# Cosformer attention into an MLP mixer on one core: the second batch's front re-ordered over three engines, num further from kv, and separate PSUM tiles for the last chunk's halves

## The chip, the core and the metric

The kernel runs on one core of a Trainium2 chip. A core has TensorE (PE; its weight loads are shown as PEld), VectorE (DVE), ScalarE (ACT), GpSimd (POOL) and SyncE (SP, which here only issues DMAs). Each engine works through its own queue in order and waits on semaphores for the others. The metric is the device time of one execution in microseconds; less is better.

## The reference

Inputs are q, k, v of (8 batches, 8 heads, 576 positions, 64) and four weights. Cosformer attention is linear attention with features `[relu(x) cos, relu(x) sin]` of width 128:

```python
kv  = einsum('bhsf,bhsd->bhfd', phi(k), v)        # 128 x 64 a head
z   = phi(k).sum(over s)
num = einsum('bhsf,bhfd->bhsd', phi(q), kv)
den = einsum('bhsf,bhf->bhs', phi(q), z) + 1e-6
x   = (num / den), heads side by side             # 576 x 512
u   = x + (relu(x.T @ w_tok1) @ w_tok2).T         # token mixing, 256 wide
out = u + relu(u @ w_ch1) @ w_ch2                 # channel mixing, 1536 wide
```

Inputs, weights and output are float32; matmul operands are bf16.

## The kernel before, in words

**Tiling.** A batch's 576 positions are four chunks of 128 (`ci` 0 to 3) and a tail of 64 (`ci` = R = 4); the tails of two batches share 128 partitions. Chunks are taken in `ORDER` 0, 1, 2, R, 3 from num on.

**Stages.** A batch has a *front* (class `Front`) and a *channel* (class `Channel`). Front: `k_side` and `q_side` make the features (two instructions a chunk, cosine and sine, L264 on DVE or L262 on ACT); `values` casts v into `v_aug`, which has a column of ones (L275 ACT, L277 DVE); q is transposed, for batches 0 and 1 by eight PE transposes and a copy (`q_trans`, L343, L347, L349), later by a DMA (`q_trans_dma`, L353); `kv` accumulates eight heads a chunk in one tile of two PSUM banks (L321) and `kv_out` copies the two halves to SBUF (L332); `num` multiplies (L362) and divides on DVE (L370 to L372); `mix_head` and `mix_tail` do w_tok1 (L385); `tok2` does w_tok2 and adds x (L409, L412), and casts to bf16 on ACT (L416, or L414 for the tail); `u_trans_dma` and `tail_trans_dma` (L438, L443) transpose u for the channel. Channel: twelve `c_step`s (relu(u @ w_ch1), L524 on PE, L528 on ACT; odd batches also do the two tails, L544), then `o_step`s of two matmuls each (L557), an addition on DVE (L562) and a store (L564).

**Interleaving.** The order of every queue is the order in which the Python calls are made. While batch b's channel runs, the front of batch b+1 is emitted in between: `pieces` makes a plan of (slot, what, chunk), where slot i is emitted after step i of the channel. C counts the twelve c steps (0 to 11), O the o steps (from 12). Batch 0's front runs alone (`first_front`) and leaves a special channel: its first three c blocks are done ahead, its `tok2` is not needed for the channel's input (which is built by matmuls), only for the final addition, and is emitted in slots 3 to 7.

**PSUM.** Two pools: `ps_mm`, four one-bank buffers (c, o, u, b), and `ps_at`, two buffers of two banks (kv, num, transposes).

**Loads.** All loads of q, k, v, all stores and all DMA transposes from batch 1 on are issued by SP in program order. Batch 2's k, v and q with their tails are issued after step 12 of batch 0's channel, behind a weight load. Batch 3's k follows at step 30.

The changed places are `values`, `kv_out`, `pieces`, `o_step` and the loop over batches at the end:

## Time and profile before

| | |
|---|---|
| median of 3 runs | 275.5 us (274.75 to 275.74) |
| the profiled execution | 275.3 us, span 273.5 us, granted clock 0.999 |
| PE / DVE / ACT / POOL busy | 263.8 / 163.8 / 128.8 / 9.6 us |
| matmul of 512 columns, between starts | 0.216 us |
| DVE feature, 128x512 (L264) | 0.45 to 0.48 us; 0.39 to 0.40 between starts |
| v cast on ACT, 128x512 (L275) | 0.59 us |
| copy of transposed q, 128x1024 | 1.00 us on ACT, 0.69 on DVE |
| k, q, v load of 1 MB, issue to landing (median) | 6.6, 9.0, 7.0 us |

How to read it: a timeline row has the start and the length in us, the engine, the source line, the operation and its operands, how many rows are merged, and in brackets the idle time of the engine before it and who ended it. Lengths of PE rows overlap, since matmuls are pipelined; the distance between starts is what a matmul costs. "SPq" rows are the issue of a DMA; its landing comes later. Batch 0's front ends at about 24 us, its channel runs to 60.3 us, batch 1's channel to about 93 us, and the following channels take about 28 (even) and 33 us (odd) each.

### The profile page before, as it was taken

The page shows a single profiled execution, that of the slowest core. Times are in us where ns is not written, and L with a number is a line of the kernel's source. Part 1 is how long each engine was busy: PE and PEld are TensorE (multiplying, and loading weights), DVE is VectorE, ACT ScalarE, POOL GpSimd, SP SyncE. Part 2 cuts the span into 40 slices and gives each one's busy share as a digit, 9 for nine tenths or more (in the row PEclk, how much of TensorE's full clock was granted, in tenths as well). Part 3 has the DMA queues.
Part 4 walks back from the last instruction along what each step waited for, and adds up shares of the span by engine and source line. Part 5 has one row for each costly group of instructions (what it writes and reads, how often), then busy time and mean ns, then how long its engine had stood idle before and what let it go on. Part 6 is the DMA issues. An engine that isn't in the chain of part 4 may idle for free.

```text
span 273.5 us, 5131 instructions
## 1 busy us (share of the span) xinstructions
PE 263.8 (96%) x2050; PEld 139.3 (51%) x2050; DVE 163.8 (60%) x374; ACT 128.8 (47%) x232; POOL 9.6 (4%) x22
## 2 busy tenths in 40 slices
PE   7989989989999999999999999999999999999993
PEld 3665446336654454446644455446644455445542
DVE  6963896779366467559366567759465666720121
ACT  4965871167616273347616272446615462525400
POOL 6400200000000000000000000000000000000000
PEclk9999999999999999999999999999999999999999
DMA  7999999968993989969784969579974371260032
GB/s 222 347 266 294 310 185 292 355 177 224 186 334 100 258 135 233 284 155 280 185 286 111 276 165 285 168 170 269 219 248 115 115 133 23 60 193 0 2 115 78
DMA packets 91816, 53.69 MB, mean 196 GB/s; under 512 B 59408, under 2 KB 86928, under 8 KB 91792
## 3 DMA queue, kind: packets, MB, share of 16 engines
q1 hardware_dynamic: 88432, 49.62, 66.3%
q0 software_dynamic: 2832, 3.21, 7.1%
q10 hardware_dynamic: 528, 0.52, 0.6%
q8 instruction: 16, 0.26, 0.4%
q14 instruction: 8, 0.07, 0.1%
HBM read 35.85 MB, written 9.44 MB: 166 GB/s over the span
## 4 chain that ended last, share of the span: by engine, by line
PE 85%; DVE 6%; ACT 3%; DMA 3%; issue 1%; POOL 0%; POOLq 0%; ACTq 0%
PE o_ps L557 31%; PE c_ps L524 24%; PE b_ps L385 6%; PE u_ps L409 6%; PE ct_ps L544 4%; PE idle_ps L205 4%; PE num_ps L362 3%; PE kv_ps L321 3%; DMA qpT<-qp 2%; DVE kp L264 1%; ACT qpT L347 1%; DMA uT<-u_bf 1%; ACT h1T L528 1%; DVE x_sb L372 1%; PE c_ps L534 1%
## 5 line engine op out<-in xcount | busy, mean ns | idle before, releaser
L557 PE MATMUL o_ps<-w_ch,h1T 128*128 128x512 bf16 (+1 forms) x396 | 95.1, 372 | 0.5 <-DVE o_sb L562 0.5
L524 PE MATMUL c_ps<-uT,w_ch 128*128 128x512 bf16 (+2 forms) x384 | 92.5, 372 | 0.9 <-DMA uT<-u_bf 0.9
L528 ACT ACTIVATE h1T<-c_ps 128x512 bf16<-128x512 f32 x93 | 55.5, 599 | 57.9 <-PE c_ps L524 57.7
L557 PEld LDWEIGHTS <-h1T 128*128 128x128 bf16 x396 | 37.1, 98 | 40.0 <-issue 1.5
L524 PEld LDWEIGHTS <-w_ch 128*128 128x128 bf16 x384 | 33.1, 97 | 30.1 <-DMA uT<-u_bf 1.4
L562 DVE TENSOR_TENSOR o_sb<-o_ps,u_sb 128x512 f32<-128x512 f32 (+1 forms) x33 | 22.2, 673 | 37.7 <-PE o_ps L557 35.7
L412 DVE TENSOR_TENSOR u_sb<-u_ps,x_sb 128x512 f32<-128x512 f32 x32 | 22.1, 689 | 9.7 <-PE u_ps L409 9.6
L416 ACT CAST u_bf<-u_sb 128x512 bf16<-128x512 f32 x28 | 17.3, 618 | 17.6 <-DVE u_sb L412 17.6
L390 ACT ACTIVATE B<-b_ps 128x512 bf16<-128x512 f32 x8 | 4.8, 597 | 39.6 <-PE b_ps L385 39.5
L409 PE MATMUL u_ps<-B,w_tok 128*128 128x512 bf16 x80 | 22.8, 379 | 0.1
L372 DVE TENSOR_TENSOR x_sb<-num_ps,den 128x512 bf16<-128x512 f32 x28 | 19.4, 691 | 1.0
L370 DVE TENSOR_SCALAR den<-num_ps 128x8 f32<-128x8 f32 (+1 forms) x35 | 5.8, 166 | 23.3 <-PE num_ps L362 23.1
L544 PEld LDWEIGHTS <-w_ch 128*128 128x128 bf16 x192 | 14.0, 98 | 9.2
L385 PE MATMUL b_ps<-x_sb,w_tok 128*128 128x512 bf16 x64 | 17.9, 379 | 0.0
L544 PE MATMUL ct_ps<-uT_tail,w_ch 128*128 128x128 bf16 x192 | 17.2, 219 | 0.0
L264 DVE TENSOR_SCALAR qp<-qt,cos_t 128x512 bf16<-128x512 f32 (+1 forms) x35 | 16.1, 459 | 0.6 <-DMA qt<-in_q_dram 0.6
L264 DVE TENSOR_SCALAR qp<-qt,sin_t 128x512 bf16<-128x512 f32 (+1 forms) x35 | 15.8, 451 | 0.0
L275 ACT CAST v_aug<-vt 128x512 bf16<-128x512 f32 (+1 forms) x28 | 15.7, 590 | 0.1
L362 PEld LDWEIGHTS <-qpT 128*128 128x128 bf16 x256 | 11.6, 98 | 7.6 <-issue 2.1
L264 DVE TENSOR_SCALAR kp<-kt,cos_t 128x512 bf16<-128x512 f32 x32 | 15.2, 479 | 0.4 <-DMA kt<-in_k_dram 0.4
L362 PE MATMUL num_ps<-kv_sb,qpT 128*128 128x65 bf16 x256 | 13.5, 193 | 1.4 <-DVE x_sb L372 0.5
L562 DVE TENSOR_TENSOR o_sb<-o_ps,u_tail 128x512 f32<-128x512 f32 x4 | 2.8, 692 | 19.2 <-PE o_ps L557 19.2
(93 smaller groups left out, 227.9 us busy)
## 6 DMA issues: line engine op xcount, KB each, us to landing
out_dram<-o_sb SPq DMA_DIRECT2D x31, 256.0 KB, 3.0
kt<-in_k_dram SPq DMA_DIRECT2D x7, 1024.0 KB, 6.6
qt<-in_q_dram SPq DMA_DIRECT2D x7, 1024.0 KB, 9.0
vt<-in_v_dram SPq DMA_DIRECT2D x7, 1024.0 KB, 7.0
w_ch<-in_moe_w_ch_dram POOLq DMA_DIRECT2D x4, 384.0 KB, 10.0
w_ch<-in_moe_w_ch_dram POOLq DMA_DIRECT2D x3, 512.0 KB, 8.3
out_dram<-o_sb SPq DMA_DIRECT2D x10, 128.0 KB, 2.3
qtt<-in_q_dram SPq DMA_DIRECT2D x8, 128.0 KB, 7.0
```

The source lines that it names most:

```text
L264: nc.vector.tensor_scalar(o_ap, i_ap, scalar1=w, scalar2=0.0, op0=ALU.mult, op1=ALU.max)
L362: nc.tensor.matmul(num_ps[:, g, j * DP:j * DP + D1], self.qT_of(ci, h), self.kv_sb[g][:, j, 0:D1], start=True, stop=True)
L372: nc.vector.tensor_mul(self.x_of(ci)[rows].rearrange("p (g j d) -> p g j d", g=2, j=HH), nv[:, :, :, 0:D], den.to_broadcast([rows.stop - r ...
L385: nc.tensor.matmul(self.b1_ps[mi], w, self.x_of(ci), start=(ci == ORDER[0]), stop=(ci == ORDER[-1]))
L409: nc.tensor.matmul(u_ps, w_tok2[:, ki, ci * P:(ci + 1) * P], self.B1[:, ki, :], start=(ki == 0), stop=(ki == NT - 1))
L412: nc.vector.tensor_add(u, u_ps[rows], self.x_of(ci)[rows])
L416: nc.scalar.copy(self.ub[:, ci, :], u)
L524: nc.tensor.matmul(c_ps[:, lo:hi], w_ch1[:, ki, mi * P:(mi + 1) * P], uT[:, lo // P:hi // P, ki, :], start=(ki == 0), stop=(ki == NCC - 1))
L528: nc.scalar.activation(self.h1T[:, mi, :], c_ps, AF.Relu)
L544: nc.tensor.matmul(self.ct_ps[:, mi % R, :], w_ch1[:, ki, mi * P:(mi + 1) * P], self.tail.uT[:, ki, :], start=(mi % R == 0 and ki == 0), s ...
L557: nc.tensor.matmul(o_ps, h, w_ch2[:, ki, cols], start=ki == 0, stop=ki == NCH - 1)
L562: nc.vector.tensor_add(o_sb, o_ps, u)
```

## The change

Five edits.

1. *Batch 1's front.* In `pieces` the plan for `first` is new. k features go to slots 4 to 7, q features 0 to 2 and transposes 0 and 1 to slots 8 to 10, and everything else up to kv stands in slot 11, the last c slot: q features 3 and R with their sine on ACT, transposes 2, 3 and R alternating with batch 0's `tok2` of chunks 2, 3 and R (now from `ps_mm`), v casts of chunks 0 and 1 on GpSimd, 2 and 3 on ACT, R on DVE, all of kv, and `kv_out`. Batch 0's `tok2` 0 and 1 go to slots 5 and 7. The nums move from O+4, 6, 7, 9, 10 to O+1, 3, 5, 7, 9, `mix` from O+11 to O+10, and the last `tok2` and the DMA transposes one slot earlier. Transposes 2 and R are copied on DVE, the others on ACT.
2. *kv_out* copies half 0 on ACT and half 1 on DVE, for every batch (before: both on ACT; batch 1 both on DVE), and in batches 2 to 7 stands one slot earlier, in the slot of the last kv.
3. *num of odd batches* from batch 3 on: the third, fourth and fifth num, `mix`, `tok2` and the transposes move one slot later.
4. *o_step* of the last batch's last chunk, done in two column halves, takes a PSUM tile for each half instead of one for both.
5. *Load of batch 2's q* (with its two tails) is issued after step 28 instead of step 12, behind the stores and DMA transposes of the steps between, with no wait on the weight load of its own.

```diff
-                nc.vector.tensor_copy(dst, src)
+                eng.tensor_copy(dst, src)
...
-        def kv_out(self, halves=(0, 1), eng=None):
-            copy = nc.scalar.copy if eng is None else eng.tensor_copy
+        def kv_out(self, halves=(0, 1)):
             for g in halves:
+                copy = nc.vector.tensor_copy if g else nc.scalar.copy
...
             if first:
-                plan = [(C + at, KS, ci, 0 < ci < R) for ci, at in enumerate((3, 4, 5, 5, 6))]
-                plan += [(C + at, QS, ci) for ci, at in enumerate((6, 7, 8, 8, 9))]
-                plan += [(C + at, QT, ci, (0, H), nc.vector if ci == R else nc.scalar)
-                         for ci, at in enumerate((9, 10, 11, 12, 13))]
-                plan += [(C + at, V, ci, nc.vector) for ci, at in enumerate((10, 11, 11, 11, 11))]
-                plan += [(O + at, KV, ci) for ci, at in enumerate((1, 1, 1, 2, 2))]
-                plan.append((O + 2, self.kv_out, (0, 1), nc.vector))
+                last = NCH - 1
+                plan = [(4, KS, 0), (5, KS, 1, True), (6, KS, 2, True), (6, KS, 3, True), (7, KS, R),
+                        (8, QS, 0), (9, QS, 1), (9, QT, 0), (10, QS, 2), (10, QT, 1)]
+                plan += [(last, *what) for what in (
+                    (QS, 3, True), (QT, 2, (0, H), nc.vector), (before.tok2, 2, None, False),
+                    (QS, R, True), (QT, 3), (before.tok2, 3, None, False),
+                    (QT, R, (0, H), nc.vector), (before.tok2, R, None, False))]
+                plan += [(last, V, ci, eng) for ci, eng in enumerate(
+                    (nc.gpsimd, nc.gpsimd, nc.scalar, nc.scalar, nc.vector))]
+                plan += [(last, KV, ci) for ci in range(NSC)]
+                plan.append((last, self.kv_out))
+                plan += [(5, before.tok2, 0, ps_at, False), (7, before.tok2, 1, ps_at, False)]
...
-                plan.append((C + (7 if odd else 8), self.kv_out))
+                plan.append((C + (6 if odd else 7), self.kv_out))
             if first:
-                at, mix, t = (O + 4, O + 6, O + 7, O + 9, O + 10), O + 11, O + 14
+                at, mix, t = (O + 1, O + 3, O + 5, O + 7, O + 9), O + 10, O + 14
             elif odd:
-                at, mix, t = (C + 8, C + 9, C + 10, C + 11, O + 2), O + 3, O + 7
+                at, mix, t = (C + 8, C + 9, C + 11, O + 1, O + 3), O + 4, O + 8
...
-            plan += [(t + at, T, ci) for ci, at in enumerate((0, 1, 2, 3, 3))]
-            plan += [(t + 2, self.u_trans_dma, 0, 3), (t + 3, self.u_trans_dma, 3, R)]
+            plan += [(t + at, T, ci) for ci, at in enumerate((0, 1, 2, 3, 3) if not first else
+                                                             (0, 0, 1, 2, 2))]
+            plan += [(t + 3 - first, self.u_trans_dma, 3, R)]
+            plan.append((t + 2 - first, self.u_trans_dma, 0, 3))
...
-            if lo == 0 and cols.start == 0:
+            if lo == 0:
                 self.o_ps[ci] = ps_mm.tile([P, Dm], F32, name="o_ps", tag="mm")
...
             if b == 0 and i == NCH:
-                load_batch(2, "kvq", behind=w_ch2_done[1])
+                load_batch(2, "kv", behind=w_ch2_done[1])
+            if b == 0 and i == NCH + 16:
+                load_batch(2, "q")
```

9 lines of the change are left out of this document (3 added, 6 removed).

## The prediction

> **What bounds the kernel now.** I read the page first, then the chain of waits in order of time, then the timeline engine by engine wherever the chain leaves TensorE (PE).
>
> ```profile
> PE 263.8 (96%) x2050; PEld 139.3 (51%) x2050; DVE 163.8 (60%) x374; ACT 128.8 (47%) x232; POOL 9.6 (4%) x22
> ...
> PEclk9999999999999999999999999999999999999999
> ...
> PE 85%; DVE 6%; ACT 3%; DMA 3%; issue 1%; POOL 0%; POOLq 0%; ACTq 0%
> ```
>
> PE sets the end, at a granted clock of 0.999. No PE work is added or removed, so the change is worth exactly the PE stalls that it takes away or makes. I measure a stall as the distance between two matmul starts, less the undisturbed distance: 0.216 us for 512 columns, 0.45 for a chunk's eight transposes, 0.243 for eight kv and 0.25 for eight num matmuls. From 26.6 us to the end, all stalls over 0.04 us:
>
> ```profile
> 39.71 0.61 PE L343 MATMUL qT_ps<-ident,qp 128*128 128x128 bf16 x8 [0.35 <-ACT qpT L347]
> ...
> 42.01 0.89 PE L321 MATMUL kv_ps<-v_aug,kp 128*128 128x65 bf16 x24 [0.30 <-ACT qpT L347]
> ...
> 50.08 0.38 PE L385 MATMUL b_ps<-x_tail,w_tail 128*128 128x512 bf16 x1 [0.26 <-DVE x_tail L372]
> ...
> 60.34 2.79 PE L524 MATMUL c_ps<-uT,w_ch 128*128 128x384 bf16 x24 [0.88 <-DMA uT<-u_bf]
> ```
>
> (a) Stage of batch 0 up to kv, 34.8 to 42.0: 0.21 + 0.07 + 0.41 + 0.51 + 0.51 + 0.47 = 2.17 us, transposes and kv behind their copies. From kv to 60.34: 0.20 + 0.42 + 0.26 + 0.11 + 1.05 = 2.04 (nums too close, then the wait for uT).
>
> ```profile
> 163.00 0.66 ACT L332 CAST kv_sb<-kv_ps 128x260 bf16<-128x260 f32 x2
> ...
> 163.43 0.56 PE L362 MATMUL num_ps<-kv_sb,qpT 128*128 128x65 bf16 x8
> ...
> 104.02 0.42 PE L362 MATMUL num_ps<-kv_sb,qpT 128*128 128x65 bf16 x8 [0.22 <-DMA qpT<-qp]
> ```
>
> (b) In the fronts of batches 3, 5 and 7 the first num waits for the copies of kv, which stand on ACT behind a relu: 0.26 + 0.16 = 0.42 each. Batch 3 loses 0.39 more to a late transposed q.
>
> ```profile
> 267.66 0.42 DVE L562 TENSOR_TENSOR o_sb<-o_ps,u_sb 128x256 f32<-128x256 f32 x1 [0.62 <-PE o_ps L557]
> 268.14 1.47 PE L557 MATMUL o_ps<-w_ch,h1T 128*128 128x256 bf16 x12 [0.52 <-DVE o_sb L562]
> ```
>
> (c) The last half chunk waits 0.57 for the addition that reads the other half of its tile. Batch 1's stage, 60 to 93, has no stall.
>
> **The change, part by part.** Sums are against the profiled execution's 275.3 us (span 273.5 and 1.8 around it), 0.2 under the median 275.5.
>
> *Batch 1's front up to kv.* The order of instructions gives each queue. PE starts c3 at 26.59 as before; seven c blocks (0.864) and two u (0.43) end at 33.50. The first transposes need q features 0, which DVE reaches at 32.66, after u_sb1; two at 0.396 would end by 33.5, two at the 0.65 spacing that the same kind shows at 33.38 and 34.04, while POOL issues its w_ch2 loads, by 33.95. I take a stall of 0.25. Then PE does T0, c10, T1, c11, T2, u2 by 37.3. T3 needs its sine on ACT, behind T0 copy, h, T1 copy, h (0.90 + 0.49 + 0.90 + 0.49 from 34.4, then a sine of 0.80): 38.0, so 0.8 lost. T3, u3, TR, uR end at 39.8.
>
> kv 0 and 1 need POOL's two casts. They start when vt lands, at 35.6. No cast on POOL is in the trace; below, half of its 0.95 us memset of 1024 elements gives 0.48, above, four times its 0.29 us select of 128 gives 1.16. Even 2.3 us for both ends at 37.9, two before kv: cost nothing. What hides them is PE's way to kv, and then the wait of kv 2; past 41.9 each microsecond would be one lost. kv 2 and 3 need casts on ACT that are queued behind ub_tail, and that waits for DVE: T_R copy until 40.45, u_tail until 41.1; ub_tail 0.53, casts 0.53 and 0.59: 42.3 and 42.8. PE came to kv 2 at 40.3, so 2.0 + 0.3 are lost, and kv ends at K = 43.4. (With DVE undelayed 43.15, delayed 43.6.) Stalls up to kv: about 3.4 where there were 2.17.
>
> *From kv to the next stage.* The kv copies: ACT, and then DVE, since the order has DVE wait for ACT's copy: 0.2 + 0.38 + 0.05 + 0.38 + 0.05 = 1.06 after K; four o matmuls and half a num (0.99) hide all but 0.08. Nums now come every 1.11 (four o, one num), just over DVE's 1.03 to 1.07 for one (0.20 + 0.24 + 0.60 to 0.67): 0.20 and 0.42 go. B is ready at K + 9.99, u reaches it at K + 10.1: 0.26 and 0.11 go. Third u_bf at K + 13.25; a uT transfer lands 3.3 later (56.98 to 60.29), so the next stage starts at S = K + 16.7, and PE has waited 0.75 instead of 1.05. S = 60.1 against 60.34: **-0.25** (0 to -0.5).
>
> *q of batch 2 behind the transposes.* This moves three DMAs past two stores and three transposes on SP. Before, q was issued at 47.73 and landed 8.3 us later, long ahead. Now it follows transposes of 1.51, 1.23 and 1.22 us (4.2 with gaps) from K + 13.3, so at K + 17.5 = S + 0.8. The next k load, two stores and the qpT transposes queue behind it. For a 1 MB load the rows next to it (kt and vt with nothing ahead of them) give 6.0, 6.2, 6.0, 6.4 and 6.6 to landing, behind another load 8.3 to 10.0; I take 6.2 since nothing stands ahead: S + 7.0. DVE is in order: q features 0 stand ahead of k features 3, which are ready 1.74 later (four at 0.396, write and signal) at S + 8.74. PE wants them for kv 3 at S + 7.93 (68.27 in the trace): 0.8 lost. The DVE half of kv_out stands behind fourteen features: S + 7.03 + 5.54 + 0.44 = S + 13.0, wanted at S + 12.6: 0.4 lost; the first qpT, behind k and two stores (2.7 + 0.7 + 0.7 + 0.7 for qtt, then 0.9), at S + 12.7, lies inside it. The second may cost 0 to 0.7; I take 0.2. **+1.4** (0 to +2.8).
>
> *kv_out a step earlier, half on DVE, later nums in odd fronts.* kv of batch 5 ends at 161.44; ACT's copy stands behind one relu until 161.9 and ends at 162.3, DVE's at 162.7; num comes at 163.17. Both waits go: 2 x 0.42 = **-0.84**. In batch 3 the next num waits for qpT, landed at 103.97, anyway: **-0.2** (0 to -0.8). Mix and uT move one slot (0.43) later; the closest uT, of batch 7, landed 1.1 ahead of use: nothing. Even fronts had no stall, and DVE is free 0.65 or more before num there. Batch 0's half on DVE ends when ACT's did (0.38 each).
>
> *Own banks for the last halves.* **-0.57**.
>
> Sum: 275.3 - 0.25 + 1.4 - 0.84 - 0.2 - 0.57 = **274.8 us**.
>
> **A rule weighed.** DVE's features slowed from 0.48 to 0.64 and 0.72 us while POOL issued loads at 32.28 to 34.51. The Trainium skill (SBUF — State Buffer, Who interferes with whom) says that DVE and GpSimd share a port pair, that a DVE cast or tensor_scalar in a two-port mode and a GpSimd instruction exclude each other, and that the first holds it for its whole length. By that, the last cosine before T3 would wait behind both casts until 37.9 and end at 38.4, T3 would be 0.4 later, and the sum 275.2; the rows here show only a slowing of 0.26 an instruction.
>
> **The rivals.**
> 1. Slower: q of batch 2 lands as late as queued loads did (8.3 to 9.0 us; 10.0 at most). For it: k of batch 3 is issued 2.6 us after it, and the page's median for qt is 9.0. Against: nothing is ahead of it. Every microsecond over 6.2 falls on kv 3: 276.9 to 277.6. It makes the change a loss from 6.9 us on, and one of over 0.5% from 8.3.
> 2. Faster: q lands in time. At 5.4 us (512 KB took 4.6 to 5.2) kv 3 does not wait and only the 0.4 at num are left, at 5.0 nothing: 273.4 to 273.8, so 273.6. For it: the rings are almost idle then. Against: no 1 MB row is under 6.0.
> 3. The odd fronts gain nothing, because DVE's half waits for ACT's half, which a relu still holds: 275.6. The order shows the wait; the times above leave 0.4.
> 4. POOL's casts outlast their cover. Each must take over 3.1 us, nearly three times my upper bound; at 4.5 us the second ends at 44.6 and kv at 45.6: 277.0. Against: all of POOL's rows but its loads are under 1 us.
>
> **How the numbers follow.** Chances: forecast 0.40, rival 1 0.20, rival 2 0.27, rival 3 0.06, rival 4 0.07. About 0.5% (1.4 us) is what a measurement of this kernel tells from no change: 274.1 to 276.9 around the median. A third of the forecast's own spread (274.0 to 275.8: batch 3's 0.6 down and 0.2 up, K's 0.25, qpT's 0.5 up) I put under 274.1. Faster: 0.13 + 0.27 = 0.40. Slower: 0.20 + 0.04 = 0.24. Same: 0.36. The range runs from 273.0 (rival 2 with batch 3's whole gain) to 277.2 (the middle of rival 1).
>
> **What would show it.** Right: kv 2 of batch 1 waits 2 us for an ACT cast, with ub_tail ahead; DVE idles between k features 2 and q features 0 of batch 2, and kv 3 there starts 0.8 late; no wait ahead of the first num of batches 5 and 7; the last twelve matmuls follow without a stop. Wrong: the stage of batch 1 without a stall, or casts on POOL of over 2 us, or kv of batch 1 ending before 42.5.

## The result and the profile after

The changed kernel takes 276.7 us (median of 11 runs, 275.45 to 278.54) where the kernel before takes 275.5 (11 runs, 274.75 to 275.91): ratio 1.0056, 95% interval 1.0032 to 1.0081. It is slower by 0.56%. The forecast was 274.8; the time lies inside its range and on the other side of no change. Three of the 11 executions had a mean granted clock of 0.993 to 0.994 and took 278.1 to 278.5; the other eight have a median of 276.55.

The first profile is of the execution that took 275.45 (span 273.6), the shortest of the 11. These are the lines of its page that answer to those of before: busy time, granted clock and the engines of the chain that ended last.

```profile
PE 261.6 (96%) x2050; PEld 138.7 (51%) x2050; DVE 164.7 (60%) x375; ACT 129.8 (47%) x229; POOL 11.2 (4%) x24
...
PEclk9999999999999999999999999999999999999999
...
PE 80%; DMA 7%; DVE 7%; ACT 2%; issue 1%; SPq 0%; DVEq 0%
```

PE has no more work than before. In the chain its share fell from 85% to 80%, and that of DMA rose from 3% to 7%: transfers have come into the path. The places, in order of time, from the timeline of PE (start, length, engine, line, operation, merged rows, and in brackets the idle time and who ended it):

```profile
34.44 0.62 PE L343 MATMUL qT_ps<-ident,qp 128*128 128x128 bf16 x8 [0.68 <-DVE qp L264]
...
38.76 0.62 PE L343 MATMUL qT_ps<-ident,qp 128*128 128x128 bf16 x8 [0.65 <-ACT qp L262]
...
42.95 0.92 PE L321 MATMUL kv_ps<-v_aug,kp 128*128 128x65 bf16 x16 [1.65 <-ACT v_aug L275]
...
69.03 0.42 PE L321 MATMUL kv_ps<-v_aug,kp 128*128 128x65 bf16 x8 [0.38 <-DVE kp L264]
...
73.70 0.42 PE L362 MATMUL num_ps<-kv_sb,qpT 128*128 128x65 bf16 x8 [0.75 <-DMA qpT<-qp]
...
243.80 2.55 PE L531 MATMUL c_ps<-uT,w_ch 128*128 128x512 bf16 x11 [0.61 <-DMA uT<-u_bf]
...
263.76 6.24 PE L564 MATMUL o_ps<-w_ch,h1T 128*128 128x512 bf16 x40
```

The first three are batch 1's front: T0, T3 and kv 2. The next two are batch 2's front: kv 3 and the first num. The sixth is new: batch 7's channel waits for its transposed u. The last row shows the end without a stop. No row of a first num in batches 5 and 7 has a bracket any more.

Beside it stands the same kernel profiled a second time (277.25 us, span 275.4; run e1 below). The table divides the spans by the starts of the channels, read from the timeline of PE: from batch 0's first mix matmul (L385) to batch 1's channel, then the length of each channel, with the next batch's front in it.

| stretch | before | forecast | after, first | after, second |
|---|---|---|---|---|
| start to batch 0's mix | 18.87 | no change | 18.76 | 19.55 |
| batch 0's mix to batch 1's channel | 41.47 | -0.25 | 41.80 (+0.33) | 41.98 (+0.51) |
| channel 1 (front of batch 2) | 32.79 | +1.4 | 34.26 (+1.47) | 34.35 (+1.56) |
| channel 2 (front of batch 3) | 28.31 | -0.2 | 27.78 (-0.53) | 28.01 (-0.30) |
| channels 3 and 5 | 32.75, 32.75 | no change | 32.74, 32.75 | 32.75, 32.75 |
| channel 4 (front of batch 5) | 27.91 | -0.42 | 27.47 (-0.44) | 27.47 (-0.44) |
| channel 6 (front of batch 7) | 27.91 | -0.42 | 28.25 (+0.34) | 28.74 (+0.83) |
| channel 7 to the last matmul | 26.59 | -0.57 | 25.92 (-0.67) | 25.92 (-0.67) |

Two stretches went against the forecast, batch 1's front and channel 6; channel 1 came out as forecast. The two profiles of one kernel differ by 0.8 in the start, which the change doesn't touch, and by 1.0 in stretches whose end waits for transfers. Over all twenty profiles of this document the start runs from 18.76 to 19.55, with a median of 19.0, so the first profile has the shortest start and the second the longest.

### The profile page after: what moved, and what is told of

Its sections match the earlier page's. It is cut to its first block, busy times and chain, and to the rows that moved or that the text cites. A ratio compares the mean times of both kernels' runs of the same rounds, so it can differ in the third digit from the quotient of the medians.

```text
span 273.6 us, 5130 instructions
## 1 busy us (share of the span) xinstructions
PE 261.6 (96%) x2050; PEld 138.7 (51%) x2050; DVE 164.7 (60%) x375; ACT 129.8 (47%) x229; POOL 11.2 (4%) x24
## 4 chain that ended last, share of the span: by engine, by line
PE 80%; DMA 7%; DVE 7%; ACT 2%; issue 1%; SPq 0%; DVEq 0%
PE o_ps L564 31%; PE c_ps L531 23%; PE b_ps L385 6%; PE u_ps L409 5%; PE num_ps L362 4%; PE ct_ps L551 4%; DMA qpT<-qp 4%; PE kv_ps L321 3%; DVE qp L264 2%; DMA uT<-u_bf 2%; DMA qt<-in_q_dram 2%; DVE kp L264 2%; PE idle_ps L205 1%; PE c_ps L541 1%; DVE u_sb L412 1%
## 5 line engine op out<-in xcount | busy, mean ns | idle before, releaser
L385 PE MATMUL b_ps<-x_sb,w_tok 128*128 128x512 bf16 x64 | 17.9, 379 | 0.0
L275 ACT CAST v_aug<-vt 128x512 bf16<-128x512 f32 (+1 forms) x30 | 16.7, 586 | 0.1
L321 PE MATMUL kv_ps<-v_aug,kp 128*128 128x65 bf16 x256 | 12.5, 193 | 2.2 <-ACT v_aug L275 1.7
```

What stands on the lines that cost most here:

```text
L321: nc.tensor.matmul(self.kv_ps[g][:, j * DP:j * DP + D1], self.k_of(ci)[:, g * HH + j, :, :] .rearrange("p a b -> p (a b)"), self.va[:, ci, ...
L385: nc.tensor.matmul(self.b1_ps[mi], w, self.x_of(ci), start=(ci == ORDER[0]), stop=(ci == ORDER[-1]))
```

## The experiments

Each run is given by median and runs, and by its ratio to the kernel before on the same chip. Theory D says that transfers have come into the path. Theory C says that the wait at kv 2 makes the chip grant TensorE less clock for a while.

### The changed kernel again (e1)

The edit: none.

> The changed kernel once more, with nothing altered, for a second profile and a second set of times. In its first profile the stalls of PE add up to a time of 275.45 us, while its median was 276.7; this run is to catch what differs between executions. Theory D (a DMA has come into PE's path): the times scatter between 275.4 and 277.5, and where a profile is longer than the first (span 273.6), its extra time stands at waits that end with a DMA: kv 3 of batch 2 behind q (0.55 before), the num of batch 2 behind the transposed q (0.91), the transposed u of batch 7 (0.78); the granted clock is 1.00. Theory C (the clock): the extra time, up to 2 us, stands in matmuls at a longer distance than 0.216 us, in one window shortly behind the stalls that PE has ahead of kv in batch 1 (33 to 43 us), where the row of the granted clock shows less than 9; the mean granted clock is 0.993 to 0.996.

277.33 us (12 runs, 276.57 to 278.52), ratio 1.0057 [1.0027, 1.0087]; two executions had a clock of 0.994. The timeline of PE in its profile:

```profile
70.37 0.42 PE L321 MATMUL kv_ps<-v_aug,kp 128*128 128x65 bf16 x8 [0.74 <-DVE kp L264]
...
74.77 0.42 PE L362 MATMUL num_ps<-kv_sb,qpT 128*128 128x65 bf16 x8 [0.47 <-DMA qpT<-qp]
...
245.59 1.69 PE L531 MATMUL c_ps<-uT,w_ch 128*128 128x512 bf16 x7 [1.11 <-DMA uT<-u_bf]
```

kv 3 waits longer than in the first profile (0.74 against 0.38), num less, the transposed u longer (1.11 against 0.61); the clock is 1.00. This is theory D's picture, with 0.8 at the start that no theory had.

### One part of the change at a time (e12, e4, e6, e5)

e12 is the kernel before with batch 1's new front alone, which the sum had at -0.25.

```diff
+                last = NCH - 1
+                plan = [(4, KS, 0), (5, KS, 1, True), (6, KS, 2, True), (6, KS, 3, True), (7, KS, R),
...
+                plan.append((last, self.kv_out, (0, 1), True))
...
-                at, mix, t = (O + 4, O + 6, O + 7, O + 9, O + 10), O + 11, O + 14
+                at, mix, t = (O + 1, O + 3, O + 5, O + 7, O + 9), O + 10, O + 14
```

> The kernel before with batch 1's new order of pieces alone (its copies on three engines, batch 0's tok2 among them, its nums and transposes one slot earlier); q of batch 2 early, kv_out, the odd batches and the last chunk as before. My sum had -0.25 for it: 275.2. The profiles have the next stage start later instead of earlier, counted from batch 0's mix: 39.8 and 40.0 in the changed kernel and 40.2 with q early, where the kernel before has 39.5; so +0.3 to +0.75, and with three executions in ten at a lower clock the median may gain 0.3 more: 275.7 to 276.5.

276.48 us (12 runs, 274.89 to 278.11), ratio 1.0022 [0.9994, 1.005]; four executions had a clock of 0.991 to 0.994. From batch 0's mix to batch 1's channel it takes 41.63, 0.16 more than before; the other stretches are within 0.23 of before. That profile is of one of the shortest executions (275.02). The eight executions at full clock have a median of 275.65, 0.4 over the kernel before on the same chip (275.27), and the four at a lower clock raise the median by 0.8 more. So the front looks like a loss, not the small gain of the sum, though its ratio's interval still touches no change.

e4 is the kernel before with own tiles for the last halves and the earlier, split kv_out.

```diff
+                copy = (eng.tensor_copy if eng is not None else
+                        nc.vector.tensor_copy if g and len(halves) == 2 else nc.scalar.copy)
...
-                plan.append((C + (7 if odd else 8), self.kv_out))
+                plan.append((C + (6 if odd else 7), self.kv_out))
...
-            if lo == 0 and cols.start == 0:
+            if lo == 0:
```

> The kernel before with two parts of the change alone: an own PSUM tile for each half of the last chunk, and in batches 2 to 7 the copies of kv one slot earlier, the second half on DVE. Batch 1's front, the nums of odd batches and the loads stay as before. My sum's terms: -0.57 at the end, -0.42 each in batches 5 and 7, -0.2 in batch 3 (0 to -0.8): 273.9, between 273.5 and 274.5, against 275.5. If the earlier copy only moves a wait (the next num then waits for DVE, since the nums are not spread), one or both of the 0.42 stay and the time is 274.3 to 274.9. If DVE's half holds up other DVE work, even batches lose up to 0.4 each and the time is 275 or over.

273.88 us (12 runs, 273.3 to 275.31), ratio 0.9923 [0.9891, 0.9954]: the number forecast. In its profile the end has -0.68, and batches 5 and 7 have -0.41 each; batch 3 has -0.04 instead of -0.2, and batch 1's front, which the edit doesn't touch, -0.18. The first nums of batches 5 and 7 start without a wait although the nums stand as before, so the shift of the odd batches was not needed for this gain.

e6 is the kernel before with the late load of q alone.

```diff
-                load_batch(2, "kvq", behind=w_ch2_done[1])
+                load_batch(2, "kv", behind=w_ch2_done[1])
+            if b == 0 and i == NCH + 16:
+                load_batch(2, "q")
```

> The kernel before with the late load of batch 2's q alone. By the changed kernel's rows the late q costs 0.55 + 0.91 = 1.46 in one profile, 0.91 + 0.63 = 1.54 in the other, and taking it back moved the median by 2.0. Theory: 275.4 + 1.5 to 2.0 = 276.9 to 277.4, with waits at kv 3 and at a num of batch 2 that end with the load of q and its transpose. Rival: the transposes of batch 1 stand later in this kernel's order than in the changed one, so q is issued later still, up to 1 us: 278. Other rival: the cost belongs to the changed front, and here it is under 0.5.

281.86 us (6 runs, 281.18 to 283.47), ratio 1.024 [1.0215, 1.0265]: a miss by over 4 us. SP's queue in its timeline shows what was overlooked:

```profile
57.13 1.39 SPq L438 DMA_TRANSPOSE uT<-u_bf  x1
58.57 0.57 SPq L86 DMA_DIRECT2D qt<-in_q_dram  x1
59.19 1.38 SPq L92 DMA_DIRECT2D qtt<-in_q_dram  x2
60.67 0.57 SPq L564 DMA_DIRECT2D out_dram<-o_sb  x1
61.33 3.08 SPq L438 DMA_TRANSPOSE uT<-u_bf  x1
```

Batch 1's last transposes are one step later in the old front, so step 28 puts the 1 MB load of q between the two transposes of u. The second lands at 67.43, and PE waits for it:

```profile
67.47 1.44 PE L524 MATMUL c_ps<-uT,w_ch 128*128 128x128 bf16 x12 [4.77 <-DMA uT<-u_bf]
```

That q lands at 65.41 and the store behind it at 66.93, so here a transpose that stands behind a 1 MB load in SP's order landed behind it. And all six executions had a clock of 0.987 to 0.994. The windows of the same profile (stretch, its length, busy time and rows of PE, PEld, DVE, ACT, POOL, then granted clock, DMA share, GB/s):

```profile
65.00:66.00 1.00, 0.00 (x0) 0.00 (x0) 0.56 (x2) 0.00 (x0) 0.00 (x0) 0.71 1.72 263
66.00:67.00 1.00, 0.00 (x0) 0.00 (x0) 1.00 (x3) 0.00 (x0) 0.00 (x0) 0.50 0.99 138
...
72.00:73.00 1.00, 1.00 (x11) 0.59 (x9) 0.00 (x0) 0.12 (x1) 0.00 (x0) 0.88 1.23 252
```

PE stands still from 62.7. Some 2.7 us later the clock falls to 0.50 and stays there until about 72.2, and matmuls of 512 columns then stand 0.427 apart instead of 0.216. Channel 1 is 7.19 longer than before: 4.9 for the stall, and 2.3 for the matmuls at half clock behind it.

e5 is the changed kernel without the one-slot shift of the odd batches.

```diff
-                at, mix, t = (C + 8, C + 9, C + 11, O + 1, O + 3), O + 4, O + 8
+                at, mix, t = (C + 8, C + 9, C + 10, C + 11, O + 2), O + 3, O + 7
```

> The changed kernel with the one-slot shift of the odd batches' later nums, mix, tok2 and transposes undone, nothing else. My sum had that shift at nothing; the two profiles of the changed kernel show the channel of batch 7 waiting 0.78 and 1.27 for the transposed u, where the kernel before had no wait. Theory (a store has come between the two transposes because of the shift): the wait goes, and as the run with the early copies of kv and unshifted nums had no wait ahead of the nums of batches 5 and 7, nothing comes back: 0.8 to 1.3 less, 275.6 to 276.4 where the changed kernel has 276.7 and 277.3. Rival: the late q of batch 2 has shifted the queue of transfers for good, and batch 7 waits for the transposed u all the same: 276.7 to 277.3.

276.62 us (12 runs, 275.13 to 278.54), ratio 1.0057 [1.0034, 1.008]. In its profile channel 6 is 27.50 and the wait for batch 7's transposed u is gone, as expected; the ratio is the changed kernel's all the same. Five of the twelve executions had the lower clock (277.0 to 278.5); the other seven have a median of 276.3, where the other runs of the changed kernel have 276.55 and 277.19. The same edit is cleaner between two kernels without such executions, e3 and e11 below: ratios 0.9985 and 0.996, 0.7 less (the intervals, [0.9957, 1.0012] and [0.9932, 0.9988], overlap). So the profiles show the wait come and go with the shift, and the medians bear out its price only weakly. Why the shift costs it is in SP's queue: in the changed kernel a store stands between the two transposes of u, in the kernel before it does not. The changed kernel:

```profile
238.12 2.05 SPq L438 DMA_TRANSPOSE uT<-u_bf  x1
240.27 0.52 SPq L571 DMA_DIRECT2D out_dram<-o_sb  x1
241.23 1.20 SPq L438 DMA_TRANSPOSE uT<-u_bf  x1
```

The kernel before:

```profile
237.41 3.21 SPq L438 DMA_TRANSPOSE uT<-u_bf  x2
240.74 1.20 SPq L443 DMA_TRANSPOSE uT_tail<-ub_tail  x1
```

The second transpose, issued at 239.43 before and at 241.23 now, lands at 243.76 instead of 241.78, with channel 7 due at 243.0. The two traces differ by 0.71 at the start of channel 6, so the issue has to be counted back from the moment at which channel 7 could start (242.75 before, 243.03 now): it stood 3.32 ahead of it and now stands 1.80 ahead. Of these 1.52, 0.43 is the slot, 0.96 the time from the begin of the store to the second issue, and 0.13 the first transpose's longer issue.

### Repairs of the changed kernel, one at a time (e2, e3)

e2 loads batch 2's q after step 12 again.

```diff
-                load_batch(2, "kv", behind=w_ch2_done[1])
-            if b == 0 and i == NCH + 16:
-                load_batch(2, "q")
+                load_batch(2, "kvq", behind=w_ch2_done[1])
```

> The changed kernel with batch 2's q loaded after step 12 again, behind k and v, as in the kernel before. My sum had +1.4 for the late q; the first profile of the changed kernel shows 0.55 ahead of kv 3 and 0.91 ahead of the first num of batch 2. Theory D: both waits go, and with them the scatter, the median falls by 1.5 to 2.3 us, from 276.7 to 274.4 to 275.2, at or under the kernel before's 275.5. Theory C: the same 1.5 go in every execution, but executions with a granted clock of 0.993 to 0.994 that are some 2 us longer stay as frequent as they were (3 of 11). Rival: q takes the rings from k and v again, so that k and v of batch 2 land later and the front of batch 2 waits for them instead; then the median stays within 0.5 of 276.7.

275.28 us (12 runs, 274.48 to 276.79), ratio 0.9983 [0.9954, 1.0012], 2.05 under e1 beside it. Channel 1 is back at 32.78. The executions with a lower clock did not go: four of twelve, 275.9 to 276.8.

e3 issues the v casts of batch 1 ahead of the last two tok2.

```diff
-                    (QS, R, True), (QT, 3), (before.tok2, 3, None, False),
-                    (QT, R, (0, H), nc.vector), (before.tok2, R, None, False))]
-                plan += [(last, V, ci, eng) for ci, eng in enumerate(
-                    (nc.gpsimd, nc.gpsimd, nc.scalar, nc.scalar, nc.vector))]
+                    (QS, R, True), (QT, 3), (V, 0, nc.gpsimd), (V, 1, nc.gpsimd),
+                    (V, 2, nc.scalar), (V, 3, nc.scalar), (before.tok2, 3, None, False),
+                    (QT, R, (0, H), nc.vector), (before.tok2, R, None, False),
+                    (V, R, nc.vector))]
```

> The changed kernel with batch 1's v casts (two on POOL, two on ACT) issued right behind the transpose of chunk 3, ahead of batch 0's last two tok2 with their casts on ACT; the cast of the tail stays last on DVE. So ACT's v casts no longer stand behind ub_tail, which waits for DVE. The first profile has 1.82 ahead of kv 2 and 0.28 ahead of kv 3. My sum's reading: both go, and as the next stage then starts earlier by as much, less what the transposed u takes back (0 to 0.6), the median falls by 1.5 to 2.1, to 274.6 to 275.2. Theory D: that and no more; the scatter stays. Theory C: without the 1.82 the stretch ahead of kv has no stall over 0.85, the executions with a lower granted clock vanish, and the median falls by 2.1 to 3, to 273.7 to 274.6.

275.5 us (12 runs, 274.74 to 276.59), ratio 0.9985 [0.9957, 1.0012], 1.83 under e1. kv of four chunks now goes through with small gaps (0.63 in all):

```profile
41.08 1.56 PE L321 MATMUL kv_ps<-v_aug,kp 128*128 128x65 bf16 x32
```

No execution had a clock under 0.998. The median agrees with the sum's reading, the clocks with theory C.

### The stall and the clock (e9, e10, e18)

e9 does the two v casts on ACT again, so that kv 2 waits longer; e18 does three more, with `(2, 3, 2)` in the same place.

```diff
+                plan += [(last, V, ci, nc.scalar) for ci in (2, 3)]
                 plan += [(last, KV, ci) for ci in range(NSC)]
```

e10 puts matmuls where PE waits.

```diff
+            ps = ps_mm.tile([P, Dm], F32, name="fill_ps", tag="mm")
+            for k in range(8):
+                nc.tensor.matmul(ps, w_tok2[:, 0, 0:P], before.B1[:, 0, :],
+                                 start=(k == 0), stop=(k == 7))
...
+                plan += [(last, KV, 0), (last, KV, 1), (last, self.fill, before)]
+                plan += [(last, KV, ci) for ci in range(2, NSC)]
```

> The changed kernel with the two v casts on ACT in batch 1 done twice in a row (the same values again), so that kv 2 waits 1.13 us longer: about 2.95 instead of 1.82, and nothing else is different. So far mean clocks of 0.993 to 0.994 came up in 14 of 47 executions of kernels with the 1.82 at kv 2, in 3 of 52 of the kernel before, and in none of 36 executions of kernels with early v casts or the old front; an execution with such a clock took some 1.5 us more than the others of its kernel. Theory C (a long stall of PE in this place makes the throttle grant less clock for a while): with 2.95 most executions or all have a clock of 0.994 or lower, and the median is 1.1 + 1.0 to 1.7 over the changed kernel's 276.7 to 277.3: 278.8 to 280.0. Theory D (only transfers in the path): the clocks stay as they were, about three in ten, and the median is 277.8 to 278.4.

278.05 us (10 runs, 277.23 to 279.96), ratio 1.0098 [1.0066, 1.0129]. The wait is 2.87, and five of ten executions had a clock of 0.992 to 0.994; their median is 278.95, that of the other five 277.44. More than three in ten, fewer than most: between the theories.

> The changed kernel with eight matmuls of 512 columns between kv 1 and kv 2 of batch 1, into a PSUM tile that nobody reads: 8 x 0.216 = 1.73 us of work for PE where it waits 1.82. It is added work whose result is not used. Theory C: the executions with a clock of 0.993 to 0.994 vanish, the others stay at 276.5 to 277.1, and the highest time falls from 278.5 to under 277.8; the wait at kv 2 becomes about 0.1. Theory D: three in ten have the low clock still, and the times are those of the changed kernel. If the added matmuls delay anything (a PSUM buffer), the times rise by 0.2 to 1.7.

276.23 us (12 runs, 275.82 to 277.41), ratio 1.0024 [0.9995, 1.0052]. No execution had a clock under 0.998, and the added matmuls delayed nothing: kv 2 starts 2.32 after kv 0, as in the first profile of the changed kernel. Without any drop of the clock this kernel still takes 0.96 more than the kernel before on its chip (275.27).

```profile
42.41 1.89 PE L332 MATMUL fill_ps<-B,w_tok 128*128 128x512 bf16 x8
44.23 0.92 PE L321 MATMUL kv_ps<-v_aug,kp 128*128 128x65 bf16 x16
```

> The changed kernel with three further casts of v on ACT ahead of kv 2 in batch 1 (chunks 2, 3 and 2 again, the same values): the wait at kv 2 becomes about 3.5, where it was 1.82 and, with two further casts, 2.87. Theory C: the share of executions with a granted clock of 0.994 or lower goes on rising, to seven in ten or more; in their profile the row of the granted clock falls within 2 us of the stall's end, and matmuls of 512 columns stand 0.43 apart for some microseconds there; the median is 276.5 + 1.7 + 1.5 = 279.7, between 279.0 and 280.5. Theory D: the share stays at three in ten, and the median is 278.3 to 278.8.

279.65 us (6 runs, 277.79 to 280.71), ratio 1.016 [1.0132, 1.0189]. The wait is 3.90, a little longer than meant. Five of six executions had the lower clock, and the profile is of one of them. Its windows, with the granted clock as the third number from the end:

```profile
44.50:45.00 0.50, 0.00 (x0) 0.00 (x0) 0.00 (x0) 0.50 (x2) 0.00 (x0) 1.00 1.01 358
45.00:45.50 0.50, 0.40 (x8) 0.40 (x8) 0.00 (x0) 0.05 (x1) 0.00 (x0) 0.50 1.08 383
...
47.50:48.50 1.00, 1.00 (x11) 0.57 (x10) 0.00 (x0) 0.00 (x0) 0.00 (x0) 0.54 1.07 326
```

The clock is 0.50 from 45.0 to about 48.4. In it kv's matmuls stand 0.055 apart and those of 512 columns 0.427, where 0.030 and 0.216 are usual. So theory C holds for the executions with a lower clock: the wait at kv 2 brings them (18 of 59 at 1.82, 5 of 10 at 2.87, 5 of 6 at 3.90), filling it takes them away (0 of 12), and so does removing its cause (0 of 65 over the eight runs with early v casts or, in e4, the old front). No profile caught an execution with a drop at 1.82; but half clock for 3.4 us out of 275 takes 0.006 off the mean clock, and 0.994 is what most of those executions have. One of the kernels without a drop, e8, has a wait of 2.08 ahead of batch 1's channel; six executions are too few to say that length alone doesn't decide, since at 18 in 59 all six would stay clear about once in nine times. Theory C explains the smaller part of the loss: of the changed kernel's executions at full clock, those of the two sets still have medians of 276.55 and 277.19, and e10 has 276.23. And the kernel before has such executions too, 9 of 117, at 277.8 to 279.9; where their clock falls no profile shows.

The traces' record of the clock says more about the chance. In all twenty profiles a stretch at full clock between two changes lasts a whole multiple of 3.41 us (12 of them in e18, from 4.04 to 45.00; 17 in e6, from 7.39 to 65.42), and within the run half clock lasts one or two (3.41 in e18, 6.83 in e6). The first rise lies anywhere from 4.04 to 7.39, so where a stall falls between two such instants differs from execution to execution. In e18 PE did nothing in the 3.41 us ahead of the drop; in e6 it stood still in the last 2.7 of them, and the clock fell all the same.

The Trainium skill (TensorE: Matmul & The Clock Gate, Part 1) has the array's clock at half after at least one idle window of about 3.4 us, and at full again after at least one busy one, with windows that run freely; its section on oscillation gives the rule that idle gaps of PE should stay under about 3.4 us. The 3.41 us between the changes here agree, and so does a drop that is a matter of chance. The limit does not agree: in e6 the clock fell 2.7 us into a gap, and with a gap of 1.82 us 18 of 59 executions had the lower clock, against none of 12 where the gap was filled.

### Repairs together (e11, e7, e15, e8)

e11 is e3 with e5's edit; e7 adds e2's; e15 is e7 again.

> The changed kernel with two repairs: the v casts of batch 1 early and the shift of odd batches undone, but batch 2's q still late. Against the run with all three repairs (273.0) it tells what the late q costs when nothing else is wrong. The late q costs 1.5 to 1.8 in batch 2 (kv 3 and num), and it frees the rings for the transposed u of batch 1, which then lands 3.3 us after its issue, and not 4.0 as with the early q: the wait there is 0.65 instead of 1.32. So I expect 273.0 + 1.5 to 1.8 - 0.67 = 273.8 to 274.2. If the late q costs its whole 2.0: 275.0. If the early q were no gain at all: 273.0.

274.64 us (12 runs, 273.74 to 275.67), ratio 0.996 [0.9932, 0.9988]: 0.4 over what was expected, under the 275.0 of the whole 2.0.

> The changed kernel with three repairs together: batch 2's q early again, the v casts of batch 1 ahead of the last two tok2, the shift of odd batches undone. What is left of the change is batch 1's new order of pieces, the split and earlier copies of kv, and the own tiles. If the three causes are independent, their effects add up: 277.3 - 2.05 - 1.8 - 0.9 = 272.5. Counted from the other end: the run of the kernel before with early copies and own tiles (273.9), and a front whose next stage starts 0.65 earlier (38.64 us after the first matmul of batch 0's mix there, 39.30 in the other): 273.2. I expect 272.5 to 273.4. If the waits only hand over to one another (a wait gone at kv comes back at the transposed u), 274 or over.

272.99 us (6 runs, 272.71 to 274.05), ratio 0.9918 [0.9898, 0.9937]: the effects add up.

> The kernel with the three repairs (q early, v casts early, no shift of odd batches) once more, beside the two above: 273.0 again, within 0.4.

273.11 us (6 runs, 272.69 to 273.83), ratio 0.9914 [0.9888, 0.994]. As expected.

e7 is no faster than e4 (0.9923), which has the old front. The new front, repaired, gets kv out earlier, and yet batch 1's channel starts 41.05 after batch 0's mix in e7 and 41.42 in e15, with 41.29 in e4. What ends PE's wait there is the transposed u, in e7:

```profile
60.05 2.12 PE L531 MATMUL c_ps<-uT,w_ch 128*128 128x384 bf16 x12 [1.15 <-DMA uT<-u_bf]
```

and in e11, whose q is late:

```profile
59.41 1.80 PE L531 MATMUL c_ps<-uT,w_ch 128*128 128x384 bf16 x10 [0.49 <-DMA uT<-u_bf]
```

The transpose is issued at 55.99 and 56.00. It lands after 4.0 us in e7, where q, its tails and two stores ahead of it land until 58.7, and after 3.4 in e11. The late q frees the transfers for the transposed u; this gain stands against its cost.

e8 is e7 with two more edits in the front: batch 0's first tok2 one slot later, q features 3 both on DVE.

```diff
-                    (QS, 3, True), (QT, 2, (0, H), nc.vector), (before.tok2, 2, None, False),
+                    (QS, 3), (QT, 2, (0, H), nc.vector), (before.tok2, 2, None, False),
...
-                plan += [(5, before.tok2, 0, ps_at, False), (7, before.tok2, 1, ps_at, False)]
+                plan += [(6, before.tok2, 0, ps_at, False), (7, before.tok2, 1, ps_at, False)]
```

> The run before with two more edits in batch 1's front: batch 0's first tok2 one slot later, behind the k features of chunks 2 and 3, and the sine of q's chunk 3 on DVE instead of ACT. The first is for the wait ahead of the first transposes (0.84 to 1.1 in four profiles, where my sum had 0.25): DVE stands idle for 1.0 us there behind the addition that this tok2 feeds, with k features queued behind it. The second is for the wait ahead of the transposes of chunk 3 (0.81), which the sine on ACT ends. If both go, kv ends 1.3 to 1.7 earlier and the next stage starts as much earlier: 271.0 to 272.0. If the slower features of DVE beside the casts on POOL (0.75 between starts for two of them, where 0.39 is usual) hold up the features of chunk 2, one of the two waits moves to the transposes of chunk 2: 272.0 to 272.8.

273.74 us (6 runs, 273.05 to 273.92), ratio 0.9932 [0.9915, 0.9949]: no gain. T0's wait fell from 0.97 to 0.51, T3's went, a wait of 0.85 appeared at TR, and kv ended 0.7 us earlier, counted from batch 0's mix; the transposed u was issued 0.7 earlier than in e7, at 55.52, and landed 4.8 us later behind the same stores. The wait for it grew from 1.32 to 2.08 and took the gain:

```profile
60.34 1.96 PE L531 MATMUL c_ps<-uT,w_ch 128*128 128x384 bf16 x11 [1.91 <-DMA uT<-u_bf]
```

### Late q with the work behind it in another order (e13, e14, e16, e17)

e13 is e11 with batch 2's q features, nums and what follows them one slot later; e14 is the same with e8's two edits. Against e11:

```diff
-                for ci, at in zip(ORDER, (1, 2, 3, 4, 5)):
+                for ci, at in zip(ORDER, (2, 3, 4, 5, 6) if b == 2 else (1, 2, 3, 4, 5)):
...
+            elif b == 2:
+                at, mix, t = (C + 10, C + 11, O + 1, O + 3, O + 5), O + 6, O + 10
```

> q of batch 2 late, v casts of batch 1 early, no shift in odd batches (as in the run that had 274.6), and in batch 2 alone: the q features and their transposes one slot later, so that all k features stand ahead of them on DVE, and the nums, mix, tok2 and transposes one slot later. If the cost of the late q is one of order, both waits of batch 2 (0.69 at kv 3, 1.13 at num) go but for 0 to 0.3 at num, and as the transposed u of batch 2 had landed 4.3 us ahead of its use, nothing comes later: 274.64 - 1.5 to 1.8 = 272.8 to 273.1, no worse than the kernel with q early. If it is the transfer itself, the waits only move (to the second num, or to the transposed u): 274 or over.

> The run before this one in the list with the two edits of batch 1's front that gave nothing while q was early (batch 0's first tok2 one slot later, the sine of q's chunk 3 on DVE). There kv ended 0.5 earlier but the transposed u landed no earlier, since stores behind q were still in the rings until 58.8. With q late the rings are free, so the next stage should start 0.4 to 0.6 earlier: 272.2 to 272.7. If something else holds the transposed u (its casts, or the issue of the stores), it is 272.8 to 273.3.

286.19 us (6 runs, 285.55 to 287.57; ratio 1.0393 [1.0363, 1.0422]) and 285.59 us (6 runs, 284.94 to 287.18; ratio 1.0375 [1.0345, 1.0405]): misses of 13 us, by e6's mechanism again. The last transposed q had slipped behind batch 3's v and q in SP's order. SP in e13:

```profile
74.96 0.54 SPq L86 DMA_DIRECT2D vt<-in_v_dram  x1
75.56 0.56 SPq L86 DMA_DIRECT2D qt<-in_q_dram  x1
76.21 4.51 SPq L353 DMA_TRANSPOSE qpT<-qp  x1
```

and PE:

```profile
84.50 0.62 PE L362 MATMUL num_ps<-kv_sb,qpT 128*128 128x65 bf16 x8 [5.92 <-DMA qpT<-qp]
```

The transposed u behind it came late too, with a wait of 3.90 in e13, and all twelve executions had a lower clock (0.975 to 0.988). The other half of the expectation held: kv 3 of batch 2 no longer waits. e16 and e17 keep all transposes ahead of those loads and begin the nums where the transposed q has landed. Against e13 and e14:

```diff
-                for ci, at in zip(ORDER, (2, 3, 4, 5, 6) if b == 2 else (1, 2, 3, 4, 5)):
+                for ci, at in zip(ORDER, (2, 3, 4, 5, 5) if b == 2 else (1, 2, 3, 4, 5)):
...
-                at, mix, t = (C + 10, C + 11, O + 1, O + 3, O + 5), O + 6, O + 10
+                at, mix, t = (C + 11, O + 1, O + 3, O + 5, O + 7), O + 8, O + 12
...
-            if b < B - 3 and i == NCH + (18 if b == 0 else 12):
+            if b < B - 3 and i == NCH + (18 if b == 0 else 16 if b == 1 else 12):
```

> q of batch 2 late, v casts of batch 1 early, no shift in odd batches; in batch 2 alone the q features stand one slot later (the last two in the slot of the last but one before, so that all five transposes stay ahead of the loads of batch 3's v and q), the nums begin two slots later, with mix, tok2 and the transposes of u four slots later, and the load of batch 4's k is issued four steps later, behind them. If the late q costs only by the order behind it, no wait over 0.3 is left in batch 2, and the time is 272.6 to 273.2, no worse than with q early (273.0 to 273.1). If the transfers themselves are the cost, a wait of 0.5 or more turns up at another place of batch 2 or at the transposed u of batch 2, and the time is 273.6 or over.

272.78 us (6 runs, 272.19 to 273.37), ratio 0.9885 [0.9836, 0.9935]. Channel 1 is 32.78, as with q early. Batch 2's q features start on DVE at 66.32, when q has landed, with all k features done at 63.8, and neither kv 3 nor the first num waits:

```profile
67.64 0.41 PE L321 MATMUL kv_ps<-v_aug,kp 128*128 128x65 bf16 x8
...
74.00 0.41 PE L362 MATMUL num_ps<-kv_sb,qpT 128*128 128x65 bf16 x8
```

So what the late q cost lay in the order of the work behind it, not in the transfer. From batch 0's mix to batch 1's channel e16 takes 40.43, where e7 and e15, with q early, take 41.05 and 41.42; in the medians this lead (272.78 against 272.99 and 273.11) is inside the scatter.

> The same with the two edits of batch 1's front (batch 0's first tok2 one slot later, the sine of q's chunk 3 on DVE). In the last pair of profiles the next stage started at 38.4 us after batch 0's mix with these edits, and at 38.7 without: 0.2 to 0.6 less than the run beside it, 272.2 to 272.9.

272.41 us (5 runs, 271.75 to 272.79), ratio 0.9865 [0.9816, 0.9914]: within what was expected, the lowest median of all the kernels here, 1.3% under the kernel before by the ratio and 1.1% by the medians. Its lead of 0.37 over e16 is inside the scatter, and the place is not the one expected: from batch 0's mix to batch 1's channel it takes 40.55, no less than e16's 40.43.

## Why the prediction was wrong

- **Batch 1's front, -0.25: wrong side.** Its waits were found and sized: T3 0.82 (forecast 0.8), kv 2 1.82 (2.0), kv 3 0.28 (0.3), u 0.59 (0.75). The main step that failed is "I take a stall of 0.25" at T0. It measured 0.84 and 0.98, and 0.51 to 1.27 over all seventeen profiles with this front. "DVE reaches at 32.66" was 0.72 early: DVE came to q features 0 at 33.38. Of this, 0.5 is idle time ahead of batch 0's first u_sb (about 1.0 in e1, e2 and e3) with k features queued behind. The two features themselves, which the sum had between 0.8 and 1.3, take 1.00 to 1.53 while POOL issues its loads: e8, e14 and e17 all have that tok2 one slot later, and T0 waits 0.51, 0.99 and 1.04 with features of 1.00, 1.48 and 1.53. Why they differ stays open. A second step failed in the reading: "PE starts c3 at 26.59 as before" is one matmul early. In the kernel before, c3 starts at 26.80, behind the twelve matmuls of the blocks done ahead:

```profile
24.21 2.75 PE L534 MATMUL c_ps<-uT,w_ch 128*128 128x512 bf16 x12
26.80 1.03 PE L524 MATMUL c_ps<-uT,w_ch 128*128 128x512 bf16 x4
```

So K and S are 0.21 too early, and most of the -0.25 is this slip: the forecast's own stalls in this stretch, 0.25 + 0.8 + 2.3 + 0.08 + 0.75, are 4.18, where the kernel before has 4.21. T0's 0.59 and this 0.21, less what the other waits were shorter, make the 0.58 between -0.25 and +0.33. The front is +0.33 and +0.51 in the two profiles, +0.16 in e12's.
- **q of batch 2, +1.4: right in place and size.** q landed 6.0 us after its issue in the first profile and 6.4 in the second (forecast 6.2), DVE stood idle until then, kv 3 waited 0.55 and num 0.91 (0.8 and 0.6), 0.91 and 0.63 in the second profile: 1.46 and 1.54. The 3.3 us that the sum took for the transposed u's landing held (3.30 and 3.34), but with the new front it holds only because q is late: with q early it is 4.0 (e7). Set against that gain, the profiles leave a cost of about 1 for the late q, while the medians lost 1.6 (e11 against e7, on two chips) and 2.05 (e1 against e2). The difference of 0.6 or more stays open.
- **kv_out and the odd fronts.** The -0.84 came, as e4 shows with -0.41 in each of the two channels, and batch 3's -0.2 was -0.53 and -0.30, inside its bounds; e12, which has neither edit, shows -0.23 there, so part of it is scatter. The step that failed is "Mix and uT move one slot (0.43) later; the closest uT, of batch 7, landed 1.1 ahead of use: nothing". By the rows the second transpose landed 0.97 ahead of use, and a slot is not only its own length: the store of the next step came to stand between the two transposes, and the second was issued 1.52 later, counted from when channel 7 could start, not 0.43. Cost: 0.78 and 1.27 in the profiles; in medians 0.7 (e3 against e11), but nothing clear of the scatter between the changed kernel and e5. In the profiles it is the largest miss: channel 6 came out 0.76 and 1.25 over its term, more than the whole gain of 0.46 that the terms add up to.
- **Own banks, -0.57.** Measured -0.67.
- **POOL's casts: nothing.** The two took 1.40 together, 0.70 each, inside the bounds of 0.48 and 1.16, and hid where the forecast said.
- **The clock.** No step had it. The sum took a stall to cost its own length. With the 1.82 at kv 2 three executions in ten have a lower clock and take 1.1 to 1.6 more (medians with and without it in the result, e1, e2, e5 and e12), which raises the median of the five sets by 0.1 to 0.8.

Putting the first profile's stretches in the place of the terms, 0.33 + 1.47 - 0.53 - 0.44 + 0.34 - 0.67 is +0.50, which together with a start 0.11 shorter makes the +0.38 that its last matmul is late; the second's make +1.49, and 0.68 at the start. The median of 276.7 lies between these two executions, 275.45 and 277.25. What remains open is why the middle of the executions lies nearer to the second: the start, which no edit touches, is at the two ends of its spread in these two profiles, the landings of q and of the transposed u varied as well, and two profiles can't say how often.

Of the rivals, none was what happened. Rival 1's place, q of batch 2, was where time was lost, yet not by its mechanism: q did not land late. That 276.7 lies in the range is luck: the range reaches so far up only for rival 1. And every sign of being right came true and none of being wrong, since none of them looked at T0 or at batch 7's transposed u. The chance of "same" at 0.36 and of "slower" at 0.24 look too low for a forecast in which T0 and the shifted slot were sized from durations alone, with nothing for what else stands in the queue.

**The rule weighed.** In the first profile no DVE feature began beside a cast on POOL. In e2 two did; DVE's timeline

```profile
35.48 0.83 DVE L264 TENSOR_SCALAR qp<-qt,cos_t 128x512 bf16<-128x512 f32 x1
36.23 0.83 DVE L264 TENSOR_SCALAR qp<-qt,sin_t 128x512 bf16<-128x512 f32 x1
36.98 0.47 DVE L264 TENSOR_SCALAR qp<-qt,cos_t 128x512 bf16<-128x512 f32 x1
```

and POOL's

```profile
35.41 1.37 POOL L277 CAST v_aug<-vt 128x512 bf16<-128x512 f32 x2 [0.86 <-DMA vt<-in_v_dram]
```

Each of the two features took 0.75 between starts where 0.39 is usual. The Trainium skill (SBUF — State Buffer, Who interferes with whom) lets the one exclude the other for the whole instruction. The direction agrees, against my "only a slowing of 0.26"; for the length, two features and two casts took 1.65 us from 35.41 to 37.06, less than the 2.2 they would take strictly in turn. T3 waited for its sine on ACT in all these profiles (0.81 to 0.82), so the loss of 0.72 on DVE cost nothing, as my sum had it, if for another reason.

## What to carry to other kernels

When a piece moves by a slot, list again what each DMA queue issues between the piece's own transfers: here one store between two transposes cost 0.8 us, and one 1 MB load between two transposes (e6), or two ahead of one (e13, e14), cost 5 to 6. Before a load is made late, see what stands behind it on the engines that it feeds: with its features and the nums moved behind it the late q cost nothing here, and the transposed u landed sooner. A stall of the bounding engine of 1.8 us or more may cost more than its length, through the clock; if it can't be removed, it can be filled, as in e10.

## What the runs showed of the hardware

- The granted clock of TensorE fell to 0.50 for 3.41 us (e18) and 6.83 us (e6) in stalls of 3.90 and 4.88 us, and in all twenty traces it changed within the run only at multiples of 3.41 us from its first rise. With a stall of 1.82 us among short matmuls 18 of 59 executions had a mean clock of 0.994 or less.
- The issue of a DMA transpose on SP, 1.2 to 2 us with little in flight, took 4.51 us behind two 1 MB loads (e13), and 3.08 behind one, its tails and a store (e6).
- Two casts on POOL of 128x512 from f32 to bf16 took 1.36 to 1.62 us together, and DVE features that began beside them showed 0.83 us instead of 0.47 (e2).
- Copies of the two halves of kv, one on ACT and one on DVE, ran one after the other: ACT's from 44.16, DVE's from 44.57 in the first profile, with DVE waiting for ACT's. That is the order that the program's semaphores gave, and no run tests whether the two engines could have copied at once.
